# Chunked delta-rule attention and a token-channel mixer: chunks of 64 tokens, 32x32 blocks inverted by substitution on VectorE, head pairs on block-diagonal operands

## The chip, the cores and the metric

The kernel runs on one core of one Trainium2 chip. The metric is device time in microseconds (us), the median of several runs. The engines that appear are PE (TensorE matmul), PEld (its weight loads), DVE (VectorE), ACT (ScalarE), POOL (GpSimd) and SP (SyncE, which here only issues DMAs). All matrix work is fp32, and an fp32 matmul shows in the trace as two instructions, each with its weight load.

## The reference

```python
def _attn_ref(q, k, v, beta):                  # B, H, S, D = 4, 8, 768, 48
    k_n = k / (np.linalg.norm(k, axis=-1, keepdims=True) + 1e-06)
    state = np.zeros((B, H, D, D))
    for t in range(S):
        y[:, :, t] = einsum('bhd,bhde->bhe', q[:, :, t], state)
        v_old = einsum('bhde,bhd->bhe', state, k_n[:, :, t])
        state = state + beta_t * einsum('bhd,bhe->bhde', k_n[:, :, t], v[:, :, t] - v_old)
def _moe_ref(x, w_tok1, w_tok2, w_ch1, w_ch2): # x = y as (4, 768, 384)
    h = np.maximum(x.transpose(0, 2, 1) @ w_tok1, 0.0) @ w_tok2      # 768 -> 256 -> 768
    u = x + h.transpose(0, 2, 1)
    return u + np.maximum(u @ w_ch1, 0.0) @ w_ch2                    # 384 -> 1536 -> 384
```

The weights come as float64 and are rounded to fp32 by the kernel itself, bit by bit.

## The kernel before

The time loop is done in chunks of 128 tokens: 4 batches of 6 chunks, 24 in all, each with its 8 heads. Within a chunk the recurrence becomes a triangular system; its matrix (identity plus a strictly triangular, beta-weighted product of keys) is inverted for each head, and what is left is a chain of small products with the 48x48 states.

Four kinds of work are written as generators and woven into one program.

- `prep` (L262) does what needs no state: it normalises the keys (`ksq`, `ksum`, `knrm`, `kden`, `krec`, `kpad`), transposes keys and queries (`p_t`, L301), forms the triangular products (`p_g`, L313, masked into `gm`, L317) and then inverts. The inversion starts from 2x2 blocks on POOL (`off`, `w_r`, L333 to L338) and doubles the block size five times: per size one 32x32 block transpose on DVE (`t_r`, L345), 16 matmuls of 64x64 by 32 columns (`p_l`, L359), a masked eviction (`lt`, L360), 16 more matmuls (`p_wu`, L372) and a subtraction (`w_r`, L373). A last step (L399 to L416) joins the two 64x64 halves of a chunk.
- `recur` (L420) is the chain through the state: `p_b` (L432), `rhs` (L434), `p_u` (L439), `u` (L441), `p_s` (L447), the new state `st` (L454), and the output `p_y` (L464, L469) into `xb`.
- `mixer` (L476) is the second half of the reference for one batch: `p_1` (L483), `p_h` (L495), then for 256 tokens at a time 12 groups of three matmuls of 128x128 by 256 columns (`p_c`, L517) and 24 of 128x128 by 384 (`p_o`, L529).
- `load_weights` reads 34 pieces of the weights and rounds each with six DVE operations and a POOL addition.

A table of due times (`at(...)`, L562 to L573) orders the program, and the instruction scheduler may move an instruction ahead of others that are not ready. The result is one fixed order for each engine. Attention of batch 0 has nothing beside it but the weights; attention of batches 1 to 3 runs beside the mixer of the batch ahead; the last mixer runs alone.

Of the kernel before, what the change touches and what calls it, by code (L numbers as in the profile page):

```python
# [9 lines left out]
FP32 = mybir.dt.float32  # L10
# [4 lines left out]
C = 128  # L15
DP = 64
R = 64
# [4 lines left out]
def kernel(  # L22
# [26 lines left out]

    nc = tc.nc  # L50
# [11 lines left out]
    GT = 256  # L62
    NG = S // GT
    GC = GT // C
    assert S % GT == 0 and DM % 128 == 0 and DTOK % 128 == 0 and DCH % 128 == 0
    assert D <= DP and H == 8 and BH <= 128

    const = ctx.enter_context(tc.tile_pool(name="const", bufs=1))
    loads = ctx.enter_context(tc.tile_pool(name="loads", bufs=3))
# [6 lines left out]
    def ps_att(shape, name):  # L76
        return psum.tile(shape, FP32, name=name, tag="att", bufs=3)

    def ps_seq(shape, name):
        return psum.tile(shape, FP32, name=name, tag="seq", bufs=2)  # L80
# [7 lines left out]
    mask_u = const.tile([128, 128], FP32, name="mask_u")  # L88
    make_upper_triangular(nc, mask_u, val=1.0, diag=False)

    def pairs(t, s):

        return t.rearrange("p h (n two s) -> p h n two s", two=2, s=s)

    def halves(t, s):

        return t.rearrange("p h (n s) -> p h n s", s=s)

    def folded(name, full, width):

        t = const.tile([128, width], FP32, name=name)
        nc.gpsimd.tensor_copy(out=t, in_=full[:, 0:width])
        for lo in range(width, full.shape[-1], width):
            nc.gpsimd.tensor_tensor(
                out=t, in0=t, in1=full[:, lo : lo + width], op=ALU.add
            )
        return t

    ident_r = folded("ident_r", ident, R)


    mask_f = const.tile([128, 64], FP32, name="mask_f")
    nc.gpsimd.memset(mask_f, 1.0)
    for sign in (1, -1):
        nc.gpsimd.affine_select(
            out=mask_f, in_=mask_f, pattern=[[-2 * sign, 64]], base=0,
            channel_multiplier=sign, compare_op=ALU.is_ge, fill=0.0,
        )
    mask_1 = folded("mask_1", mask_f, R // 2)
# [18 lines left out]
    for i in range(2):  # L138
# [466 lines left out]
```

## Time and profile before

| | |
|---|---|
| median of 3 runs | 1270.54 us (1268.54 to 1272.89) |
| the profiled execution | 1278.59 us, of which the span of the trace is 1276.8 us |
| PE busy | 1169.6 us, 92% of the span |
| DVE, POOL, ACT busy | 431.3, 197.0, 180.7 us |
| packets moved by DMA | 83395, mean 26 GB/s |

A busy time is the union of an engine's instructions. PE's matmuls are pipelined, so a busy PE is not PE at its peak. The granted clock of TensorE has two levels, 1.2 and 2.4 GHz, and a mean of 0.74 in a stretch is a mixture of the two. Until the first record of the clock (at about 80 us here) the column shows 1.00, whatever the level.

### The profile page before, as it was taken

The numbers are of one execution on the slowest core, as the hardware profiler recorded it, in microseconds if no ns is written. First come the engines' busy times: TensorE is split into PE (matmuls) and PEld (weight loads), VectorE is DVE, ScalarE is ACT, GpSimd is POOL, SyncE is SP. The second block draws the span as 40 slices with busy tenths as digits, with TensorE's granted clock in tenths as the row PEclk, the third lists the DMA queues.
The fourth block names the chain that finished last, engine by engine and source line by source line (L and its number), as shares of the span: only waits on it lengthen the run. The fifth ranks groups of instructions, "written<-read, shape, count | busy, mean of one in ns | idle before, by whom it ended". The sixth has DMA issues, their size and how long they took to land.

```text
span 1276.8 us, 27386 instructions
## 1 busy us (share of the span) xinstructions
PE 1169.6 (92%) x12462; PEld 920.6 (72%) x12462; DVE 431.3 (34%) x898; ACT 180.7 (14%) x407; POOL 197.0 (15%) x295
## 2 busy tenths in 40 slices
PE   4788787788999999999999999999999999999998
PEld 3767676677787777777677777777677777786776
DVE  6766674332334323322322313322323322211000
ACT  2001011011111120120121120220121120111111
POOL 6233141111111110110110110110111110000000
PEclk9986575776999999899897998999799999799999
DMA  6232230010001000100000100100000000000000
GB/s 123 79 85 77 70 89 25 14 26 8 15 14 26 21 13 15 32 13 14 20 14 8 32 14 14 32 14 14 20 14 8 14 1 8 7 1 13 13 13 13
DMA packets 83395, 33.31 MB, mean 26 GB/s; under 512 B 75824, under 2 KB 78896, under 8 KB 83280
## 3 DMA queue, kind: packets, MB, share of 16 engines
q1 hardware_dynamic: 83280, 31.56, 10.2%
q8 instruction: 98, 1.61, 0.5%
q14 instruction: 17, 0.14, 0.0%
HBM read 26.84 MB, written 4.72 MB: 25 GB/s over the span
## 4 chain that ended last, share of the span: by engine, by line
PE 86%; DVE 8%; POOL 4%; issue 2%; ACT 0%; POOLq 0%; ACTq 0%
PE p_c L517 15%; PE p_o L529 15%; PE p_l L359 12%; PE p_wu L372 12%; PE p_g L313 4%; PE p_u L439 4%; PE p_y L469 4%; PE p_h L495 3%; PE p_t L301 3%; PE p_l L410 2%; PE p_wu L415 2%; PE p L483 2%; DVE t_r L345 2%; PE p_x L399 2%; POOL off L333 2%
## 5 line engine op out<-in xcount | busy, mean ns | idle before, releaser
L517 PE MATMUL p_c<-u_t,wc 128*128 128x256 f32 x864 | 227.8, 405 | 0.1
L359 PEld LDWEIGHTS p_l<-t_r,gm 64*64 64x64 f32 x3840 | 144.3, 155 | 111.4 <-issue 89.4
L359 PE MATMUL p_l<-t_r,gm 64*64 64x32 f32 x3840 | 157.3, 238 | 65.0 <-DVE t_r L345 60.0
L529 PE MATMUL p_o<-wc,r 128*128 128x384 f32 x576 | 216.8, 507 | 0.0
L372 PEld LDWEIGHTS p_wu<-w_r,lt 64*64 64x64 f32 x3840 | 146.5, 158 | 56.7 <-DVE lt L360 33.0
L517 PEld LDWEIGHTS p_c<-u_t,wc 128*128 128x128 f32 x864 | 159.7, 197 | 25.5 <-issue 2.6
L372 PE MATMUL p_wu<-w_r,lt 64*64 64x32 f32 x3840 | 160.6, 240 | 14.0 <-DVE lt L360 14.0
L529 PEld LDWEIGHTS p_o<-wc,r 128*128 128x128 f32 x576 | 101.2, 191 | 50.9 <-issue 2.9
L360 DVE TENSOR_TENSOR lt<-p_l,mask 128x256 f32<-128x256 f32 x120 | 50.9, 424 | 175.2 <-PE p_l L359 175.0
L317 DVE TENSOR_TENSOR gm<-p_g,mask_u 128x512 f32<-128x512 f32 x96 | 62.0, 685 | 129.3 <-PE p_g L313 129.2
L373 DVE TENSOR_TENSOR w_r<-w_r,p_wu 128x256 f32<-128x256 f32 x120 | 50.6, 421 | 158.8 <-PE p_wu L372 158.6
L345 DVE STREAM_TRANSPOSE t_r<-w_r 128x512 f32<-128x512 f32 x120 | 85.2, 710 | 45.6 <-POOL w_r L338 43.2
L522 ACT ACTIVATE r<-p_c 128x256 f32<-128x256 f32 x144 | 55.2, 383 | 249.6 <-PE p_c L517 249.6
L405 POOL COPY w_t<-w_r 64x512 f32<-64x512 f32 x24 | 15.0, 625 | 455.0 <-DVE w_r L373 455.0
L313 PE MATMUL p_g<-kbq_t,k_t 64*128 64x256 f32 x384 | 64.3, 423 | 3.8 <-DVE gm L317 3.2
L536 DVE TENSOR_TENSOR o_sb<-p_o,xb 128x384 f32<-128x384 f32 x24 | 13.4, 557 | 135.4 <-PE p_o L529 135.4
L313 PEld LDWEIGHTS p_g<-kbq_t,k_t 64*128 64x128 f32 x384 | 41.1, 198 | 20.3 <-DVE gm L317 6.5
L411 ACT COPY lt<-p_l 64x512 f32<-64x512 f32 x24 | 13.9, 580 | 279.6 <-PE p_l L410 279.6
L469 PE MATMUL p_y<-u,gm 128*128 128x48 f32 x384 | 52.1, 289 | 0.0
L469 PEld LDWEIGHTS p_y<-u,gm 128*128 128x128 f32 x384 | 50.0, 207 | 1.9 <-issue 1.0
L333 POOL TENSOR_TENSOR off<-gm,mask 64x256 f32<-64x256 f32 x48 | 36.0, 750 | 78.0 <-DVE gm L317 76.5
L215 POOL TENSOR_TENSOR w_f<-w_f,w_r 128x384 uint32<-128x384 uint32 (+1 forms) x34 | 33.5, 986 | 91.5 <-DVE w_f L207 77.8
(89 smaller groups left out, 1076.5 us busy)
## 6 DMA issues: line engine op xcount, KB each, us to landing
d<-in_moe_w_ch_dram SPq DMA_DIRECT2D x24, 384.0 KB, 3.2
k_raw<-in_k_dram SPq DMA_DIRECT2D x24, 192.0 KB, 2.7
qpad<-in_q_dram SPq DMA_DIRECT2D x24, 192.0 KB, 2.9
v_raw<-in_v_dram SPq DMA_DIRECT2D x24, 192.0 KB, 2.6
out_dram<-o_sb SPq DMA_DIRECT2D x24, 192.0 KB, 1.9
d<-in_moe_w_tok_dram SPq DMA_DIRECT2D x6, 256.0 KB, 3.0
d<-in_moe_w_tok_dram SPq DMA_DIRECT2D x4, 384.0 KB, 3.1
beta_sb<-in_beta_dram SPq DMA_DIRECT2D x1, 96.0 KB, 2.2
```

What stands on the lines that cost most here:

```text
L313: nc.tensor.matmul(p_g[par][:, jj], k_t[lo : lo + DP, j], kbq_t[lo : lo + DP, j])
L317: nc.vector.tensor_tensor(out=gm[:, 4 * g + par : 4 * g + 4 : 2], in0=p_g[par], in1=mask_u[:, None, None, :].to_broadcast([128, 2, 2, 128] ...
L333: nc.gpsimd.tensor_tensor(out=off[lo : lo + R], in0=gm[lo : lo + R, :, 0, lo + 1 : lo + R : 2], in1=mask_1[lo : lo + R, None, :].to_broadc ...
L345: nc.vector.transpose(dst.rearrange("p h n -> p (h n)"), src.rearrange("p h n -> p (h n)"))
L359: nc.tensor.matmul(p_l[r, h], gm[r, h, 0, r], t_e[r, h])
L360: nc.vector.tensor_tensor(out=lt_e, in0=halves(p_l, s), in1=halves(masks[s][:, None, :], s).to_broadcast([128, H, half // s, s]), op=ALU.mult,
L372: nc.tensor.matmul(p_w[r, h], lt[r, h], w_o[r, h])
L439: nc.tensor.matmul(p_u[:, h], w_t[:, h], rhs[:, h])
L469: nc.tensor.matmul(p_y[:, h], gm[:, h, 1], u[:, h], start=(c == 0 and h == 0), stop=(h == H - 1), skip_group_check=True,)
L517: nc.tensor.matmul(p_c, wc1[:, cb, f * 128 : (f + 1) * 128], u_t[:, cb], start=(cb == 0), stop=(cb == NCB - 1),)
L522: nc.scalar.activation(r, p_c, ACTF.Relu)
L529: nc.tensor.matmul(p_o, r2[f][:, i * C : (i + 1) * C], wc2[:, f], start=(f == 0), stop=(f == NHT - 1),)
```

## The change

- **Chunk and unit.** Tokens still come in units of 128 (24 of them, `u`), but the recurrence goes in chunks of 64: two per unit, 48 in all.
- **Head pairs.** The two heads of a pair sit on the two halves of the partitions. One operand of each product is block-diagonal (`kbd`, `r_bd`, `w_bd`, `s_bd`, with zeros off the blocks), so that one 128-row matmul serves both heads. `recur` is three products now: `p_q` (keys and queries with the state), `p_w` (inverse with the right-hand side) and `p_s` (new state and output together), four matmuls each.
- **Inversion.** Units go in rounds of two, 12 rounds. `prep` writes the four diagonal 32x32 blocks of each matrix to DRAM (`n_dram`), `invert` reads them back with one block on each of 64 partitions (`x`), and runs 30 steps of back substitution on DVE, a product and a sum each: 60 operations, each dependent on the one before, on 30 to 240 elements per partition, 9920 elements in all. The inverse and its transpose (`xt`, by POOL) go to DRAM again, and 16 small DMAs bring them to the places where the matmuls read them (`wt`, `t11`, `w22`). `join` then makes the off-diagonal 32x32 block of each 64x64 inverse with 16 matmuls (`p_z`, `p_x`) and four ACT copies.
- **Mixer.** `p_c` takes 128 tokens at a time, four groups of 128 columns to a PSUM tile; the transposition of the next 128 tokens (`turn`) stands ahead of `p_o`.
- **Weights.** Three DVE operations per piece instead of six; two ACT operations take over the rest.
- **DMAs.** All on SP's queue, in order. There are 638 of them now; before there were 131.

```diff
-C = 128
+C = 64
+U = 128
+HB = 32
+RU = 2
...
+        nc.scalar.activation(r, lo, ACTF.Copy, scale=2.0**-29)
+        nc.scalar.square(a, hi.bitcast(FP32))
...
+        kst = work.tile([128, NP, 2, D], FP32, name="kst", bufs=1)
+        for par in range(2):
+            for cc in range(2):
+                nc.sync.dma_start(
+                    out=kst[C * par : C * par + C, :, cc],
+                    in_=kp[C * cc : C * cc + C, par::2, 0:D],
+                )
...
+        for g in range(2):
+            p_g = ps_prep([128, NB // 2, 2, C], "p_g")
+            for i in range(NB // 2):
+                nb = g * (NB // 2) + i
+                nc.tensor.matmul(p_g[:, i], kbd[0][:, nb], kqt[:, nb])
...
+        for par in range(2):
+            for i in range(2):
+                lo = (4 * j + 2 * par + i) * NB
+                row = C * par + HB * i
+                nc.sync.dma_start(
+                    out=xins[rnd][lo : lo + NB].rearrange("b s t -> s b t"),
+                    in_=gm[row : row + HB, :, 2, HB * i : HB * i + HB],
+                )
...
+    def invert(rnd):
...
+        x = work.tile([n, HB, HB], FP32, name="x")
+        nc.sync.dma_start(out=x, in_=n_dram)
+        yield
+        for s in range(1, HB - 1):
+            w = HB - 1 - s
+            tmp = work.tile([n, s, w], FP32, name="sub")
             nc.vector.tensor_tensor(
+                out=tmp, in0=x[:, 0:s, s : s + 1].to_broadcast([n, s, w]),
+                in1=x[:, s : s + 1, s + 1 : HB].to_broadcast([n, s, w]), op=ALU.mult,
+            )
+            nc.vector.tensor_tensor(
+                out=x[:, 0:s, s + 1 : HB], in0=x[:, 0:s, s + 1 : HB], in1=tmp,
+                op=ALU.add,
             )
             yield
...
+        nc.sync.dma_start(out=w_dram, in_=x)
+        nc.sync.dma_start(out=t_dram, in_=xt)
...
+    def join(u):
...
+            nc.tensor.matmul(p_z[0:65, nb], gm[:, lo : lo + 65], t11[:, nb])
...
+            nc.tensor.matmul(p_x[0:65, nb], zst[:, lo : lo + 65], w22[:, nb])
...
     def recur(t):
...
+                nc.tensor.matmul(p_q[:, p], kqt[:, 2 * p + cc], s0[:, p])
+            for r, e in heads:
+                nc.vector.tensor_tensor(
+                    out=r_bd[r, :, e], in0=v_st[r, :, cc], in1=p_q[hi, :, e],
+                    op=ALU.subtract,
+                )
...
+                p_w[0 : C + 1, p], wts[u % NV][:, w_lo : w_lo + C + 1], r_bd[:, p]
+            )
+        for r, e in heads:
+            nc.scalar.copy(w_bd[r, :, e], p_w[lo, :, e])
...
+            nc.tensor.matmul(p_s[:, p], gm[:, 2 * p + cc, 0:2], w_bd[:, p])
...
+        at(t0 - 2.9 + j, 0.08, prep, u)
+        if j == 0:
+            at(t0 - 1.4, 0.9 / (HB + 2), invert, rnd)
+        at(u - 0.9, 0, load_v, u)
+        at(t0 - 0.4 + 0.2 * j, 0.1, join, u)
+        for cc in range(2):
+            at(u + 0.5 * cc, 0.15, recur, 2 * u + cc)
```

What moves in the fixed orders is shown at three places.

PE before, beside the mixer of batch 0: the small matmuls of one inversion (`p_l`, `p_wu`) alternate with two or three matmuls of the mixer.

```order
L359 MATMUL p_l<-t_r,gm 64x32 x16
L517 MATMUL p_c<-u_t,wc_159 128x256 x2
L372 MATMUL p_wu<-w_r,lt_128 64x32 x16
L517 MATMUL p_c<-u_t,wc_159 128x256 x3
L359 MATMUL p_l<-t_r,gm 64x32 x16
L517 MATMUL p_c<-u_t,wc_159 128x256 x2
L372 MATMUL p_wu<-w_r,lt_130 64x32 x16
```

PE after, the end of the mixer's stretch between two rounds and the start of the next round's join and recurrence, beside the mixer of batch 0:

```order
L497 MATMUL p_ut<-ident,xb 128x128 x3
L528 MATMUL p_o<-wc_137,r_2845 128x384 x3
L392 MATMUL p_z<-t_0_115,gm_95 65x64 x8
L528 MATMUL p_o<-wc_137,r_2845 128x384
L528 MATMUL p_o<-wc_137,r_2892 128x384
L403 MATMUL p_x<-w_0_119,zst_123 65x64 x8
L528 MATMUL p_o<-wc_137,r_2892 128x384 x2
L442 MATMUL p_w<-r_bd_125,wt_107 65x96 x4
L528 MATMUL p_o<-wc_137,r_2892 128x384
L451 MATMUL p_s<-w_bd_127,gm_95 128x96
L392 MATMUL p_z<-t_1_116,gm_96 65x64 x8
```

The alternation is gone: a long stretch of mixer work comes first, and then the join and the four chunks of a round stand close together, with single matmuls of the mixer between them.

DVE after, in the same kind of round: the last two chunks of a round, and then the substitution of the next round.

```order
L455 TENSOR_TENSOR s_bd_130<-s_bd_129,p_s 64x4x48 x2
L461 TENSOR_TENSOR xb<-xb,p_s 64x384
L312 TENSOR_TENSOR gm_95<-p_g,mb 128x4x2x64
L429 TENSOR_TENSOR r_bd_125<-v_st,p_q 64x4x48 x2
L344 TENSOR_TENSOR sub<-x 64x30
L348 TENSOR_TENSOR x<-x,sub 64x30
L344 TENSOR_TENSOR sub<-x 64x58
L348 TENSOR_TENSOR x<-x,sub 64x2x29
```

The substitution begins behind the right-hand side (`r_bd`) of the round's last chunk, whenever its input `x` has come.

SP after, from the stores of one round's blocks to the loads that the next join waits for:

```order
L327 DMA n_dram<-gm_98 32x8x32 x4
L278 DMA kst<-kpad_86 64x4x48 x3
L339 DMA x<-n_dram 64x1024
L278 DMA kst<-kpad_86 64x4x48
L216 DMA kpad_85<-in_k_dram 128x8x48
L327 DMA n_dram<-gm_95 32x8x32 x4
L227 DMA v_st<-in_v_dram 64x4x48 x4
L216 DMA qpad_89<-in_q_dram 128x8x48
L278 DMA kst<-kpad_85 64x4x48 x4
L358 DMA w_dram<-x 64x1024
L359 DMA t_dram<-xt 64x1024
L369 DMA wt_109<-w_dram 32x8x32 x2
```

Before, the queue held nothing here but the loads of `k_raw`, `qpad` and `v_raw`, one at a time, and the stores of `o_sb`.

## Rows read from the trace of the kernel before

**Rows 1.** The page: busy time, share of the span, instructions; all DMA packets.

```profile
PE 1169.6 (92%) x12462; PEld 920.6 (72%) x12462; DVE 431.3 (34%) x898; ACT 180.7 (14%) x407; POOL 197.0 (15%) x295
DMA packets 83395, 33.31 MB, mean 26 GB/s; under 512 B 75824, under 2 KB 78896, under 8 KB 83280
```

**Rows 2.** Three stages: length, busy time and instructions per engine, granted clock, DMA.

```profile
0.00:320.00 320.00, 241.81 (x2806) 215.34 (x2806) 177.15 (x393) 35.49 (x70) 92.38 (x143) 0.74 0.24 59
320.00:1161.00 841.00, 816.22 (x9238) 626.08 (x9235) 246.88 (x492) 127.36 (x290) 104.64 (x152) 0.96 0.07 15
1161.00:1276.80 115.80, 111.58 (x427) 79.22 (x425) 7.23 (x13) 17.83 (x47) 0.00 (x0) 1.00 0.03 12
```

**Rows 3.** Groups by line: busy us, mean ns | idle before, releaser.

```profile
L517 PE MATMUL p_c<-u_t,wc 128*128 128x256 f32 x864 | 227.8, 405 | 0.1
L359 PE MATMUL p_l<-t_r,gm 64*64 64x32 f32 x3840 | 157.3, 238 | 65.0 <-DVE t_r L345 60.0
L372 PE MATMUL p_wu<-w_r,lt 64*64 64x32 f32 x3840 | 160.6, 240 | 14.0 <-DVE lt L360 14.0
```

**Rows 4.** Timeline of PE (start, length): one inversion step, early and beside a mixer.

```profile
26.04 1.92 PE L372 MATMUL p_wu<-w_r,lt 64*64 64x32 f32 x32 [0.61 <-DVE lt L360]
397.50 1.12 PE L372 MATMUL p_wu<-w_r,lt 64*64 64x32 f32 x32
```

**Rows 5.** Last mixer: timeline (first row), chain that ended last (other rows).

```profile
1168.77 8.11 PE L495 MATMUL p_h<-r,w 128*128 128x384 f32 x24
...
1210.14 15.54 PE p_c L517 x72
1225.68 15.48 PE p_o L529 x48
```

**Rows 6.** Timeline of PE: full-width weights with few columns.

```profile
1042.83 1.89 PE L439 MATMUL p_u<-rhs,w_t 128*128 128x48 f32 x16
1044.65 1.14 PE L313 MATMUL p_g<-kbq_t,k_t 64*128 64x256 f32 x8
...
431.72 1.03 PE L447 MATMUL p_s<-u,kpad 128*128 128x96 f32 x8
...
65.10 1.86 PE L447 MATMUL p_s<-u,kpad 128*128 128x96 f32 x8
```

**Rows 7.** DVE operations by tile (ns min/median/max), and a dependent pair in the timeline.

```profile
L281 DVE TENSOR_TENSOR kpad<-k_raw,krec x24: 557/559/1089, 7.3 to 1055.9; 128x384 f32<-128x384 f32 x24
L278 DVE TENSOR_SCALAR kden<-knrm x24: 126/164/784, 6.3 to 970.1; 128x8 f32<-128x8 f32 x24
L280 DVE RECIPROCAL krec<-kden x24: 159/202/203, 7.1 to 970.2; 128x8 f32<-128x8 f32 x24
L454 DVE TENSOR_TENSOR st<-st,p_s x32: 307/352/358, 124.0 to 1103.7; 64x192 f32<-64x192 f32 x32
...
1105.24 0.42 DVE L373 TENSOR_TENSOR w_r<-w_r,p_wu 128x256 f32<-128x256 f32 x1 [1.14 <-PE p_wu L372]
1105.69 0.71 DVE L345 STREAM_TRANSPOSE t_r<-w_r 128x512 f32<-128x512 f32 x1
```

**Rows 8.** Groups by line: an eviction on ACT, a copy on POOL.

```profile
L441 ACT COPY u<-p_u 128x384 f32<-128x384 f32 x24 | 11.5, 479 | 51.0 <-PE p_u L439 51.0
L405 POOL COPY w_t<-w_r 64x512 f32<-64x512 f32 x24 | 15.0, 625 | 455.0 <-DVE w_r L373 455.0
```

**Rows 9.** DMAs: SP's issue (ns, then timeline), us to landing on the page.

```profile
L251 SPq DMA_DIRECT2D k_raw<-in_k_dram x24: 367/368/1080, 1.3 to 963.9; - x24
...
4.21 0.86 SPq L251 DMA_DIRECT2D qpad<-in_q_dram  x1
79.09 34.05 SPq L193 DMA_DIRECT2D d<-in_moe_w_ch_dram  x8
...
k_raw<-in_k_dram SPq DMA_DIRECT2D x24, 192.0 KB, 2.7
out_dram<-o_sb SPq DMA_DIRECT2D x24, 192.0 KB, 1.9
```

More of the change, by code (lines that the diff above doesn't have):

```diff
@@ L87 @@
     make_identity(nc, ident)
[L88 to L107, printed above, removed]
@@ L293, in prep @@
+        bd = blocks(kbd[0])
+        nc.scalar.copy(kqt_k, p_t)
+        nc.scalar.copy(bd[0:DP, :, :, 0:C], p_t[0:DP])
+        nc.gpsimd.tensor_copy(
+            out=bd[DP : 2 * DP, :, :, C : 2 * C], in_=kqt_k[DP : 2 * DP]
         )
         yield
[L296 to L303 removed]
@@ L367, in step @@
             yield
-            p_w = ps_att([128, H, half], "p_wu")
-            for h in range(H):
-                for lo in range(0, 128, size):
-                    r = slice(lo, lo + size)
-                    nc.tensor.matmul(p_w[r, h], lt[r, h], w_o[r, h])
-            nc.vector.tensor_tensor(
-                out=w_o, in0=w_o, in1=halves(p_w, s), op=ALU.subtract
+        rnd, j = divmod(u, RU)
+        if j == 0:
+            xins[rnd] = dram.tile([RU * 4 * NB, HB, HB], FP32, name="n_dram")
@@ L393, in prep @@
-        yield from step(32, 64, w_6, t_6)
-        lo_r, hi_r = slice(0, 64), slice(64, 128)
-        p_x = ps_att([64, H, 32], "p_x")
-        for h in range(H):
-            nc.tensor.matmul(p_x[:, h], w_6[lo_r, h], lt_buf[32][lo_r, h, 0:32])
-        nc.vector.tensor_tensor(
-            out=t_6[lo_r, :, 0:32], in0=t_6[lo_r, :, 0:32], in1=p_x, op=ALU.subtract
-        )
-        w_t = work.tile([128, H, 128], FP32, name="w_t")
-        nc.gpsimd.memset(w_t[hi_r, :, 0:64], 0.0)
-        nc.gpsimd.tensor_copy(out=w_t[lo_r, :, 0:64], in_=w_6[lo_r])
@@ L406, in prep @@
-        nc.gpsimd.tensor_copy(out=w_t[hi_r, :, 64:128], in_=w_6[hi_r])
-        yield
-        p_l = ps_att([128, H, 64], "p_l")
-        for h in range(H):
-            nc.tensor.matmul(p_l[hi_r, h], gm[lo_r, h, 0, hi_r], t_6[lo_r, h])
-        nc.scalar.copy(lt_buf[64][hi_r], p_l[hi_r])
-        yield
-        p_w = ps_att([64, H, 64], "p_wu")
-        for h in range(H):
-            nc.tensor.matmul(p_w[:, h], lt_buf[64][hi_r, h], w_6[hi_r, h])
-        nc.scalar.mul(w_t[lo_r, :, 64:128], p_w, -1.0)
+        nc.vector.memset(x.rearrange("b s t -> b (s t)")[:, 0 :: HB + 1], 1.0)
@@ L437, in recur @@
[L437 to L452 removed]
+            p_q = ps_seq([128, NP, 2 * D], "p_q")
@@ new lines, in recur @@
+            for p in range(NP):
+                nc.tensor.matmul(p_q[:, p], kqt[:, 2 * p + cc], s0[:, p])
[3 more added lines that the diff above has]
+                    op=ALU.subtract,
+                )
+            nc.scalar.mul(y, p_q[lo], -1.0)
+        else:
+            for r, e in heads:
+                nc.gpsimd.tensor_copy(out=r_bd[r, :, e], in_=v_st[r, :, cc])
+        yield
@@ L462, in recur @@
         if c > 0:
[L463 to L473 removed]
+            nc.vector.tensor_tensor(out=y, in0=y, in1=p_s[lo], op=ALU.add)
+        else:
+            nc.scalar.copy(y, p_s[lo])
```

495 lines of the change are left out of this document (235 added, 260 removed).

## The prediction

> **What bounds the kernel now.** I read the page first: PE is busy for 92% of the span [rows 1], so the question is what PE does and at which clock. The stages answer it [rows 2]. In the first 320 us (attention of batch 0 and the weights) PE is busy for 242 us, at a mean granted clock of 0.74; in the next 841 us (attention of batches 1 to 3 beside mixers 0 to 2) it is busy for 816 us at 0.96; in the last 116 us (mixer 3) for 112 us at 1.00. The groups by line show what fills this [rows 3]: 7680 of PE's 12462 instructions are the 64x64 products `p_l` and `p_wu` of the inversion, 318 us of busy time, and `p_l` waits 65 us more for the transposes. One step of 32 takes 1.92 us early in the run and 1.12 us beside a mixer [rows 4]: the two levels of the clock, 1.2 and 2.4 GHz. So the middle is bound by PE's own work, the head by the chain of one inversion after another, and the tail by one mixer.
>
> **PE's work after the change, at full clock.** An instruction with a full-width weight load costs about 114 ns however few columns it has: 16 of `p_u` fill the 1.82 us between their start and the next row's, and 8 of `p_s` take about 1.0 us (1.86 us early in the run) [rows 6]. Per unit: 8 transposes and 16 instructions of `p_g`, 24 x 0.114 = 2.7 us; 32 of `p_z` and `p_x`, with 65 columns of weights, which the trace lacks: between 0.033 us (a step of 32 in about 1.05 us [rows 4]) and 0.114 us each, taken as 0.08, 2.6 us; two chunks with 16 of `p_q` and `p_s` at 0.125 and 8 of `p_w` at 0.08, 5.3 us. That is 10.6 us, 21 us per round of two units. A mixer: 48 instructions of `p_1` and `p_h`, 15.8 us (24 took 8.11 [rows 5]); per unit 24 of `p_o`, 7.7 us (48 in 15.48), and 72 of `p_c`. These have half the columns of before, so the floor is half of 215.8 ns (72 in 15.54), 108 ns, and the weight load sets 114: 8.2 us against 7.8. With 0.3 us of transposes a unit's share is 18.9 us, a round's 38. PE's floor is therefore 59 us per round; 841 us for 18 units was 93 us per two units.
>
> **The loop that replaces it.** A round cannot start before its inverse is there, and its blocks come out of the round ahead. By the orders the loop runs: join, chunks 0 to 3 up to the last right-hand side, substitution on DVE, two trips through DRAM, next join.
>
> (a) Join to the last `r_bd`. A hop between engines is 0.03 to 0.15 us in the rows [rows 7]. The join has two groups of 16 matmul instructions (1.3 us each) and two pairs of ACT copies of 256 elements; 384 take 479 ns [rows 8], so I take 0.4 each: 4.2 us. A chunk is `p_q` 1.0, two DVE operations of 0.35 (192 elements [rows 7]), `p_w` 0.65, two ACT copies of 0.32, `p_s` 1.0, two DVE operations of 0.35, and six hops: 5.3 us. Three chunks, and `p_q` and `r_bd` of the fourth: 21.8 us in all. The second join, two units' `prep` (4.6 us of PE for transposes and `p_g`) and single mixer matmuls stand between these in PE's queue; I charge 6 us of them as not hidden. 28 us.
>
> (b) Substitution. 384 elements took 559 ns, 8 elements 164 to 202 [rows 7]: 155 ns and 1.04 ns per element. A dependent operation starts 0.03 us after the end of the one ahead [rows 7]. 60 x 0.185 + 9920 x 0.00104 = 11.1 + 10.3 = 21.4 us. The low end is 10 us (the fixed part wholly hidden, which no row shows for dependent operations), the high end 27 (if short broadcast rows cost half as much again per element); I take 21.4, because the dependent pair is this very case. Between these operations DVE's order has a chunk's state and output, a key normalisation and two to six additions for the mixer, some 5 us. 26.5 us. The Trainium skill, page "VectorE: DVE Perf Modes", section "The TRN2 errata — SBUF-src ops pay a fixed extra latency per instruction", speaks against this step: many small operations pay the fixed cost each time, and tiles should have 512 elements or more. Its cycle table would give 58 cycles fixed at 0.96 GHz, an estimate of 14 us for the 60; the same section corrects this to about 150 cycles, which agrees with the 559 ns.
>
> (c) The way back. POOL's transposed copy of 1024 elements, 1.2 us (512 took 625 ns [rows 8]), the store of it (issue 0.37, landing 1.9), eight loads issued at 0.37 each, 3.0 us, and the landing of the last, 2.3, between 1.9 and 2.7 [rows 9]: 8.8 us.
>
> The way out (`gm`, four stores, a load of `x`: about 9 us) starts at `p_g`, about 14 us after the join, and is over at about 23 us, before `r_bd` of the last chunk: it costs nothing as long as (a) is longer. Where it is late, DVE's order makes the substitution later by as much. The loop is 28 + 26.5 + 8.8 = 63 us, above PE's floor of 59; with some of it at the low clock I take **64 us**. The mixer's stretch of about 28 us in PE's queue covers (b) and (c) but for a few us, so this stretch is nearly free.
>
> **The sum**, against the profiled execution. *Until the first join, 84 us.* SP issues 16 loads of beta (16 x 0.37) and four of keys and queries at about 0.9 us each, where SP is backed up [rows 9]; the first keys are there at about 10 us. Normalisation 3, two units through one `kbd` 14: 27 us. Way out 6.5, and then the substitution with ten weight pieces in between in DVE's order. Eight pieces took 34 us before [rows 9], with six DVE operations each; now there are three, so ten take between 30 and 43; I take 42 us for both together, since a piece that comes late holds the substitution behind it. Way back 8.8. *Two loops in the head* at the low clock, where (a) is 32 us: 32 + 42 + 9 = 83 with weights, and 32 + 28 + 9 = 69 without. *Nine loops* at 64: 576. *The last round's chunks* 32. *The last mixer* 109: from `p_h` to the end took 108 [rows 5], six groups of `p_c` cost 0.4 more each, and `turn` ahead of `p_o` takes away a wait or two. 84 + 83 + 69 + 576 + 32 + 109 = 953 us of span. The profiled execution was 1.8 us longer than its span and 0.6% above the median: 955 x 1270.54 / 1278.59 = 949, which I give as **950 us**.
>
> **Rivals.** (1) *PE is the bound.* If the operations of the substitution overlap, or the trips are shorter, nine loops cost 59 each and the head loses some 20 us: 953 - 45 - 20 = 888, or 884 us; 904 where the head stays. For it: floor and loop are 4 us apart. Against it: the dependent pair [rows 7].
> (2) *The low clock in the chunks.* PE waits a few us ahead of each join, and then works with gaps of 0.7 us in every chunk. The head shows what such gaps go with: steps at 1.92 us and a clock of 0.74 [rows 2, 4]; the middle, nearly without gaps, had 0.96. At 1.2 GHz the products in (a) take some 10 us longer: loops of 74, 90 us more, 1038 us. The Trainium skill ("TensorE: Matmul & The Clock Gate", part 1) says the same as a rule: the throttled clock is the default, and only sustained activity lifts it. Against it: the long stretch of mixer matmuls in each round.
> (3) *Slower than before: the small DMAs.* 18 to 22 issues of 128 to 192 byte pieces lie on each loop. The time is as before when a loop takes 100 us ((1276.8 - 84 - 83 - 69 - 141) / 9), 36 us more, nearly 2 us for each of these DMAs. This would happen if they ran one behind the other up to their landing. Against it: a load of 1024 pieces of 192 bytes is issued in 0.86 to 1.08 us where they queue up [rows 9], so 256 pieces should not need more than the 0.37 us of the issue; and 75824 of 83395 packets were under 512 bytes before [rows 1]. From 1275 us.
> (4) *The change does not do what it says.* The wide matmuls bring nothing where the weight load is the cost: this is in the sum already, at 114 ns for 48 to 128 columns.
>
> **How the numbers follow.** The forecast (loops of 61 to 69 us, 925 to 995 us) 0.50; rival 1 (865 to 925) 0.25; rival 2 (995 to 1085) 0.18; rival 3 0.03; faster than 865 by a shorter head as well, 0.04. The low end takes PE's floor and a head 35 us shorter (30 in place of 42 us in the two substitutions with weights, 11 us less in the third): 953 - 45 - 35 = 873, 867 us. The high end takes loops of 74 and a head 20 us longer (all of it at the low clock): 1065, 1058 us. Range 865 to 1060; what is left out is below 865, rival 3 and the upper part of rival 2, about 1 in 10. A measurement of this kernel tells 0.3% from no change; only rival 3 reaches that: faster 0.96, same 0.01, slower 0.03.
>
> **What would show it.** Right: PE busy near 600 to 700 us and not over 80% of the span; 720 substitution operations of 190 to 440 ns on DVE, about 250 us; joins 60 to 68 us apart once a mixer runs, with `p_z` waiting for the DMA of `t11` or `wt`; `p_c` at about 114 ns; mixer 3 about 109 us from `p_h` on. Wrong: joins 59 us apart with no wait on PE (rival 1); `p_s` at 1.8 us for 8 beside a mixer (rival 2); DMAs on SP's queue with landings well above 3 us, or the substitution waiting for `x` and not for `r_bd`; a first join far from 84 us.

## The result, and the profile after

The changed kernel takes **918.75 us** (median of 4 runs, 912.34 to 923.02); beside it the kernel before took 1271.72 us. The ratio is 0.7215, with a 95% interval of 0.7162 to 0.7268. The prediction was 950 us, range 865 to 1060. The profiled execution took 917.84 us, its span is 916.1 us. Of all executions told of below one, the longest of `warm2`, fell into a slower state at a lower granted clock, and its time is left out.

The page of the changed kernel, to be read against [rows 1]:

```profile
PE 735.6 (80%) x5034; PEld 594.5 (65%) x5034; DVE 473.3 (52%) x1254; ACT 232.5 (25%) x535; POOL 138.3 (15%) x150
...
PEclk9555875695699999999999999999999999989999
DMA packets 192354, 56.06 MB, mean 61 GB/s; under 512 B 182560, under 2 KB 185632, under 8 KB 192288
...
L348 DVE TENSOR_TENSOR x<-x,sub 64x30 f32<-64x30 f32 (+4 forms) x360 | 124.1, 345 | 9.9
L344 DVE TENSOR_TENSOR sub<-x 64x30 f32<-64x30 f32 (+4 forms) x360 | 120.3, 334 | 16.8 <-DMA x<-n_dram 7.6
```

PE has 434 us less work. The 7680 small products of the inversion are gone [rows 3], and 720 operations of the substitution on DVE (244 us) stand in their place. There are 2.3 times as many packets. The stages (length, busy time and instructions of PE, PEld, DVE, ACT, POOL, then the granted clock, DMA share and GB/s), against [rows 2]:

```profile
0.00:87.00 87.00, 16.13 (x74) 13.80 (x75) 65.31 (x149) 26.66 (x58) 43.17 (x56) 0.66 0.59 128
87.00:165.40 78.40, 29.02 (x217) 24.62 (x217) 56.06 (x135) 26.31 (x59) 24.61 (x21) 0.67 0.45 111
165.40:227.70 62.30, 29.00 (x216) 24.56 (x216) 36.11 (x100) 13.66 (x34) 9.09 (x9) 0.72 0.31 64
...
355.28:415.18 59.90, 59.16 (x421) 47.79 (x422) 34.01 (x95) 15.94 (x37) 7.16 (x7) 1.00 0.31 61
...
774.80:916.10 141.30, 131.02 (x792) 101.45 (x792) 13.14 (x28) 20.88 (x45) 0.00 (x0) 0.96 0.04 13
```

The windows are cut at the joins (the first `p_z` of a round). In the head PE is busy for a fifth to a half of the time, and DVE for three quarters while there are weights. In the middle a round of 59.90 us holds 59.16 us of busy PE at the full clock. The joins of the changed kernel and of the variants below, in us from the start of the span (each has twelve):

| kernel | joins 1, 2, 3 | mean of the nine rounds from join 3 to join 12 | last join to the end |
|---|---|---|---|
| changed kernel | 87.0, 165.4, 227.7 | 60.8 | 141.3 |
| `sub20` (ten steps less) | 69.2, 137.6, 202.2 | 54.0 | 167.5 |
| `sub40` (ten steps twice) | 87.6, 168.1, 243.8 | 64.9 | 141.0 |
| `back` (shorter way back) | 85.2, 162.1, 225.3 | 60.0 | 142.3 |
| `mix256` (256 tokens to a `p_c`) | 87.1, 165.6, 227.8 | 60.6 | 144.6 |
| `early` (inversion a unit earlier) | 85.9, 159.1, 232.5 | 54.0 | 175.6 |
| `after_w6` (six-op rounding) | 89.3, 173.7, 253.7 | 60.3 | 139.0 |
| `warm` / `warm2` (unread matmuls) | 99.4, 196.4, 282.5 / 92.9, 181.1, 252.7 | 60.1 / 60.0 | 141.3 / 141.2 |
| `best1` (inversion ahead, tuned head) | 87.8, 122.9, 196.7 | 54.5 | 175.6 |

One round on four engines (start, length). PE: the join that begins it, which waits, the mixer's last stretch, and the next join.

```profile
355.28 1.13 PE L392 MATMUL p_z<-t,gm 128*65 128x64 f32 x16 [0.72 <-DMA t<-t_dram]
...
399.40 8.20 PE L513 MATMUL p_c<-u_t,wc 128*128 128x128 f32 x72
407.44 7.91 PE L528 MATMUL p_o<-wc,r 128*128 128x384 f32 x24
415.18 1.11 PE L392 MATMUL p_z<-t,gm 128*65 128x64 f32 x16
```

DVE: the last right-hand side of the round that began at 355.28, the first operation of the substitution, a dependent pair, and the last operation.

```profile
379.94 0.74 DVE L429 TENSOR_TENSOR r_bd<-v_st,p_q 64x192 f32<-64x192 f32 x2
...
381.19 0.17 DVE L344 TENSOR_TENSOR sub<-x 64x30 f32<-64x30 f32 x1
...
394.61 0.40 DVE L344 TENSOR_TENSOR sub<-x 64x240 f32<-64x240 f32 x1
395.04 0.40 DVE L348 TENSOR_TENSOR x<-x,sub 64x240 f32<-64x240 f32 x1
...
406.46 0.20 DVE L348 TENSOR_TENSOR x<-x,sub 64x30 f32<-64x30 f32 x1
```

The way back: POOL's transposed copy, and SP's issues, of which the second load of `t11` (413.02) is the last that the first `p_z` needs.

```profile
406.73 1.96 POOL L355 COPY xt<-x 64x1024 f32<-64x1024 f32 x1 [22.18 <-DVE x L348]
```

```profile
406.69 0.48 SPq L358 DMA_DIRECT2D w_dram<-x  x1
408.71 0.48 SPq L359 DMA_DIRECT2D t_dram<-xt  x1
...
413.02 0.45 SPq L378 DMA_DIRECT2D t<-t_dram  x1
```

So this round is 25.9 us from the join to the substitution, 25.5 us of substitution, 8.5 us of way back. That is the prediction's loop. But `p_z` shows no wait at its end: PE comes out of `p_o` 2.2 us behind the issue of that load. In four of the nine rounds `p_z` waits for it, for 0.3 to 0.7 us, and starts 1.9 to 2.1 us behind the issue; so here, too, the data lands as PE becomes free. Loop and PE end together, and the trace alone does not tell which of them sets the round. The experiments were made for that, and for the head.

### The profile page after: what moved, and what is told of

Its sections match the earlier page's. It is cut to its first block, busy times and chain, and to the rows that moved or that the text cites. A ratio compares the mean times of both kernels' runs of the same rounds, so it can differ in the third digit from the quotient of the medians.

```text
span 916.1 us, 13640 instructions
## 1 busy us (share of the span) xinstructions
PE 735.6 (80%) x5034; PEld 594.5 (65%) x5034; DVE 473.3 (52%) x1254; ACT 232.5 (25%) x535; POOL 138.3 (15%) x150
## 4 chain that ended last, share of the span: by engine, by line
PE 58%; DVE 19%; DMA 7%; ACT 5%; issue 4%; POOL 3%; SPq 3%; POOLq 0%; ACTq 0%; DVEq 0%
PE p_c L513 14%; PE p_o L528 13%; DVE x L348 6%; DVE sub L344 6%; PE p_s L451 6%; PE p_q L427 4%; PE p_w L442 4%; PE p_h L487 4%; PE p_g L310 3%; PE p_z L392 3%; PE p L475 3%; PE p_x L403 3%; ACT w_bd L446 3%; DMA t_dram<-xt 2%; DMA t<-t_dram 1%
## 5 line engine op out<-in xcount | busy, mean ns | idle before, releaser
L513 PE MATMUL p_c<-u_t,wc 128*128 128x128 f32 x1728 | 202.6, 276 | 2.3 <-ACT u_t L501 2.3
L528 PE MATMUL p_o<-wc,r 128*128 128x384 f32 x576 | 196.7, 488 | 0.0
L348 DVE TENSOR_TENSOR x<-x,sub 64x30 f32<-64x30 f32 (+4 forms) x360 | 124.1, 345 | 9.9
L344 DVE TENSOR_TENSOR sub<-x 64x30 f32<-64x30 f32 (+4 forms) x360 | 120.3, 334 | 16.8 <-DMA x<-n_dram 7.6
L451 PE MATMUL p_s<-w_bd,gm 128*128 128x96 f32 x384 | 58.8, 296 | 11.1 <-ACT w_bd L446 8.6
L451 PEld LDWEIGHTS p_s<-w_bd,gm 128*128 128x128 f32 x384 | 50.5, 203 | 22.8 <-ACT w_bd L446 22.8
L310 PE MATMUL p_g<-kqt,kbd 128*128 128x128 f32 x384 | 56.8, 297 | 6.9 <-POOL kbd L292 4.7
L310 PEld LDWEIGHTS p_g<-kqt,kbd 128*128 128x128 f32 x384 | 51.1, 208 | 13.5 <-POOL kbd L292 13.3
L427 PEld LDWEIGHTS p_q<-s_bd,kqt 128*128 128x128 f32 x352 | 44.3, 194 | 17.9 <-DVE s_bd L455 5.7
L427 PE MATMUL p_q<-s_bd,kqt 128*128 128x96 f32 x352 | 49.8, 282 | 7.2 <-DVE s_bd L455 7.0
L442 PE MATMUL p_w<-r_bd,wt 128*65 128x96 f32 x384 | 43.2, 257 | 5.0 <-DVE r_bd L429 2.5
```

Source lines behind the costliest of these rows:

```text
L310: nc.tensor.matmul(p_g[:, i], kbd[0][:, nb], kqt[:, nb])
L344: nc.vector.tensor_tensor(out=tmp, in0=x[:, 0:s, s : s + 1].to_broadcast([n, s, w]), in1=x[:, s : s + 1, s + 1 : HB].to_broadcast([n, s, w ...
L348: nc.vector.tensor_tensor(out=x[:, 0:s, s + 1 : HB], in0=x[:, 0:s, s + 1 : HB], in1=tmp, op=ALU.add,)
L427: nc.tensor.matmul(p_q[:, p], kqt[:, 2 * p + cc], s0[:, p])
L442: nc.tensor.matmul(p_w[0 : C + 1, p], wts[u % NV][:, w_lo : w_lo + C + 1], r_bd[:, p])
L451: nc.tensor.matmul(p_s[:, p], gm[:, 2 * p + cc, 0:2], w_bd[:, p])
```

## The experiments

In all of them the rest of the program is the changed kernel's, except in `before_w3`. The times are medians.

**1. Ten substitution steps less.**

```diff
-        for s in range(1, HB - 1):
+        for s in [*range(1, 11), *range(21, HB - 1)]:
```

> Leaves out 10 of the 30 substitution steps (s = 11 to 20, the longest ones), so the inverse is not the inverse; all else is as in the changed kernel. A step takes 0.85 us there, so each loop has 8.5 us less on DVE. Theory A (the round is the loop: join, chunks, substitution, trip through DRAM): joins in the middle 60.8 - 8.5 = 52 us apart, the head 14 + 17 us shorter: about 811 us. Theory B (PE's own work sets the middle, with a floor of 58 to 59 us): joins 58 to 59.5 us apart, p_z without a wait, only the head falls: 870 to 890 us.

Measured: 857.99 us (857.57 to 858.32), between the two forecasts; each theory is right in one place. The joins 4 to 9 come 50.3 to 52.8 us apart, some 8 us less as the loop says, and well below the 58 us that theory B held for PE's floor. The whole is 61 us faster and not 107: the nine rounds give 6.8 us each and not 8.5, the head 26 us, and the end takes 26 back. What PE does between two joins had changed. In the round shown it ran 144 instructions of `p_c` in both kernels, but fewer of `p_o` (over the nine rounds 1152 of `p_c` for 1296, and 368 of `p_o` for 432). PE's `p_o` alone in that round (length, busy and instructions of PE and PEld), first of the changed kernel, then of this one:

```profile
355.28:415.18 59.90, 22.80 (x66) 11.85 (x66) 1.00 0.31 61
```

```profile
312.18:364.31 52.13, 15.41 (x43) 7.29 (x42) 1.00 0.36 69
```

The mixer's work that had stood between the joins is done behind the last one, 167.5 us there against 141.3. The same view of this kernel's end, with all instructions (PE, PEld, DVE, ACT, POOL):

```profile
688.30:855.80 167.50, 163.46 (x1014) 128.46 (x1012) 15.53 (x33) 25.33 (x53) 0.00 (x0) 1.00 0.05 14
```

So the fixed order lays as much mixer work between two joins as fits into the loop that it was made for, and the backlog is worked off at the end. PE's own floor, spread over the nine rounds, is by this run about (486.2 + 167.5 - 141.3) / 9 = 56.9 us.

**2. Ten steps twice.**

```diff
+            if 11 <= s <= 20:
+                again = work.tile([n, s, w], FP32, name="again", bufs=1)
+                nc.vector.tensor_tensor(out=again, in0=x[:, 0:s, s:s+1]..., in1=tmp, op=ALU.mult)
+                nc.vector.tensor_tensor(out=again, in0=again, in1=tmp, op=ALU.add)
```

> Does 10 of the 30 substitution steps (s = 11 to 20) once more, on a scratch tile, so each loop has about 8.5 us more on DVE and the result is the same. Theory A (the loop is the bound): joins in the middle 69 us apart, the whole 14 + 11 x 8.5 = about 105 us longer, 1020 to 1030 us. Theory B (PE is the bound and the loop has slack): the middle moves by less than the 8.5 us; with all the slack that the five rounds without a wait could hide (several us) joins 62 to 65 us apart, 960 to 1000 us.

Measured: 970.37 us (968.61 to 970.50), rounds of 64.9 us. That is in theory B's interval, for a reason that neither theory had. Twenty more operations of 0.39 us cost 4.1 us per round, not 8.5. DVE of this kernel:

```profile
415.10 0.39 DVE L344 TENSOR_TENSOR sub<-x 64x234 f32<-64x234 f32 x1
415.41 0.38 DVE L358 TENSOR_TENSOR again<-again,sub 64x228 f32<-64x228 f32 x1
415.72 0.39 DVE L348 TENSOR_TENSOR x<-x,sub 64x234 f32<-64x234 f32 x1
416.03 0.39 DVE L354 TENSOR_TENSOR again<-x,sub 64x234 f32<-64x234 f32 x1
416.34 0.39 DVE L344 TENSOR_TENSOR sub<-x 64x238 f32<-64x238 f32 x1
```

The operations now alternate between two chains, and each starts 0.31 us behind the one ahead, before that one has ended. In the changed kernel the same operations depend on each other and start 0.43 us apart. A step of four costs 1.24 us, a step of two 0.87: 10 x 0.37 = 3.7 us, near the 4.1 by which the rounds grew. The rounds followed DVE's chain by its real cost, so theory A's mechanism holds for a longer loop too, and its expectation was mis-sized. PE's order followed as well, though the edit adds nothing but DVE operations: in the same round it holds 164 instructions of `p_c` and these of `p_o`:

```profile
377.45:440.91 63.46, 24.91 (x72) 12.91 (x72) 1.00 0.31 61
```

**3. One part of the change alone, in the kernel before: three operations per weight piece.**

```diff
-        nc.vector.scalar_tensor_tensor(out=f, in0=lo, scalar=29, in1=f, ...)
-        nc.vector.tensor_scalar(out=r, in0=lo, scalar1=28, ...)
-        nc.vector.tensor_scalar(out=e, in0=hi, scalar1=20, ...)
+        nc.scalar.activation(r, lo, ACTF.Copy, scale=2.0**-29)
+        nc.scalar.square(a, hi.bitcast(FP32))
```

> The kernel before with one part of the change alone: three DVE operations and two ACT operations per piece of the weights, in place of six on DVE. Theory A (weights cost the head because their DVE operations stand between those of the inversion): 34 pieces with 3 operations of some 0.4 us less each, 41 us of DVE time, of which a half shows: 1245 to 1260 us. Theory B (the head of before is a chain through PE and its evictions, and the weights lie beside it): within 5 us of 1270.

Measured: 1273.95 us, ratio 0.9993 (0.9968 to 1.0017): nothing, theory B. DVE has 137.3 us of work in the first 320 us there instead of 177.2 [rows 2], and the 40 us less moved nothing, so they were not on the path.

**4. The same part undone in the changed kernel** (the same diff, backwards).

> The changed kernel with the rounding of the weights as before: six DVE operations per piece instead of three, and none on ACT. Theory A (in the head of the changed kernel DVE is the path, so what stood between its operations counts): about 24 of the 34 pieces lie between substitution operations of the first two rounds; 3 operations of 0.4 to 0.5 us more each, 30 to 35 us longer: 945 to 960 us. Theory B (as in the kernel before, where the same edit alone gave nothing: the additions on POOL and the arrival of the pieces set the pace): within 6 us of 919.

Measured: 938.28 us (937.30 to 942.99), 19.5 us slower. The three head joins come 2.3, 8.3 and 26.0 us later; some 6 us are given back behind them. So the part is worth 20 us here and nothing before; the reading is that the substitution, the other part of the change, has put DVE on the path of the head. Theory A was right in kind; it had 30 to 35 us, and the head lost 26. But not where it said: the first two substitutions hardly grew (42.8 and 39.9 us for 41.3 and 39.7). The weights ended later, the last DVE operation on them starting at 243.4 us and not at 184.9, so that they stand between the operations of the third substitution as well: it took 37.7 us, and 24.5 in the changed kernel, which has none of them there.

**5. The mixer of before.**

```diff
-                p_c = ps_mlp([128, FG, 128], "p_c")
+                p_c = ps_mlp([128, GT], "p_c")        # GT = 256
```

> The changed kernel with the mixer of before: 256 tokens to a product p_c, so half as many instructions of 256 columns. Theory A (weight load of 114 ns against 108 ns of columns, PE on the path in the middle): 1728 x 6 ns, about 10 us less PE time, 907 to 912 us. Theory B (PE is not on the path but for the last mixer): 1 to 3 us less at most; the transposition that no longer stands ahead of p_o may give that back: 915 to 922 us.

Measured: 917.95 us (914.81 to 921.57), theory B. The rounds gain 0.1 to 0.2 us, the end loses 3.3.

**6. A shorter way back.**

```diff
-        nc.gpsimd.tensor_copy(out=xt, in_=x.rearrange("b s t -> b t s"))
+        nc.vector.tensor_copy(out=xt, in_=x.rearrange("b s t -> b t s"))
```

and per unit the loads in the order four of `wt`, two of `t11`, two of `w22`.

> The changed kernel with a shorter way back: the transposed copy xt by DVE instead of POOL (1.96 us there; about 1.2 by the rate of the substitution's operations), and the loads of t11 and w22 issued ahead of those of wt (the second t11 is two places earlier, 0.9 us). Theory A (the way back is on the loop): 1.5 to 1.9 us less in each of eleven rounds, 898 to 903 us. Theory B (mixer work in PE's queue fills the round): joins in the middle move by less than 0.5 us, 912 to 917 us.

Measured: 909.12 us (905.27 to 909.94), between the two intervals. The first two joins gain 1.8 and 1.5 us, the third gives 0.8 back; the middle gains 0.8 us per round on average, almost half of it in the first. One round shows why it is not more. The last operation of the substitution ends at 400.0 us. The second `t11` is issued 5.3 us behind that (it was 6.4; it is the sixth load in both kernels, so the reordering gave less than expected). With the 2.2 us from issue to join of the changed kernel (413.02 to 415.18) it has landed by about 407.6. PE comes to `p_z` at 408.57, out of the same 24 `p_o`:

```profile
404.91 0.89 SPq L376 DMA_DIRECT2D t<-t_dram  x2
```

```profile
400.83 7.91 PE L526 MATMUL p_o<-wc,r 128*128 128x384 f32 x24
408.57 1.11 PE L390 MATMUL p_z<-t,gm 128*65 128x64 f32 x16
```

The order on PE is the one made for the longer loop (144 `p_c` and 67 `p_o` between these joins), so PE's queue sets the round now. Theory B for the middle but for its first round, theory A for the first two joins. DVE's copy took 1.06 us where POOL's took 1.96.

**7. The inversion a unit earlier.**

```diff
-        at(t0 - 2.9 + j, 0.08, prep, u)
+        at(t0 - 3.9 + j, 0.08, prep, u)
-            at(t0 - 1.4, 0.9 / (HB + 2), invert, rnd)
+            at(t0 - 2.4, 0.9 / (HB + 2), invert, rnd)
```

(the loads a unit earlier as well; the weights begin a unit earlier and are spread over a unit more; `NV = 5`, one buffer of `x`, for room)

> The changed kernel with one thing moved: loads, prep and invert are planned one unit (128 tokens) earlier, with five buffers of gm, kqt and wt instead of four (x has one buffer instead of two, for room). No operation is added or left out. Theory A (the substitution needs only keys; it is the order of the program that ties it to the chunks and makes a loop of the round, and without that PE's own work is the bound): no wait of p_z in the middle, the second and third joins come 30 to 40 us earlier together, and the whole is set by PE's work, as in the run with ten steps left out: 830 to 860 us. Theory B (the round is a loop whatever the plan, since DVE's queue, DRAM trips and buffers follow the chunks): 905 to 925 us.

Measured: 894.87 us (893.93 to 896.04), faster than theory B had it and 35 us above theory A's interval. In the middle it is theory A: `p_z` waits for 0.45 us at most, rounds are 54.0 us on average, and the mixer's backlog stands behind the last join (the last two stages, from join 4 to join 12 and from there to the end):

```profile
295.50:718.70 423.20, 415.45 (x3112) 347.44 (x3111) 259.89 (x735) 120.97 (x285) 51.71 (x52) 1.00 0.32 62
718.70:894.30 175.60, 171.55 (x1072) 135.52 (x1070) 16.79 (x36) 27.66 (x59) 0.00 (x0) 1.00 0.04 12
```

From the third join to the end it takes 661.8 us, with ten steps less it took 653.7, in the changed kernel 688.4. So the substitution is not tied to the chunks by data; `prep` and `invert` need keys and beta only. The plan had tied it. The head did not gain: the second join is 6 us earlier, but the third 5 us later. Two things in the trace make for that, and no run takes them apart. DVE's order puts the second substitution behind the state of the first chunk, for which it waits (the load of its `x` was issued at 90.37 us):

```profile
97.70 0.73 DVE L459 COPY s_bd<-p_s 64x192 f32<-64x192 f32 x2 [11.58 <-PE p_s L451]
98.47 0.18 DVE L344 TENSOR_TENSOR sub<-x 64x30 f32<-64x30 f32 x1
```

And the weights, spread further by the same edit, lie in the third substitution: their last DVE operation starts at 227.7 us instead of 184.9, and that substitution takes 51.8 us instead of 24.5.

**8 and 9. The head's clock: unread matmuls beside the first three substitutions.** First `warm`, then `warm2`; the way back has twelve more, of 512 columns of `x` and of `ident` by `ident`.

```diff
+                for _ in range(2 if s % 2 else 1):
+                    nc.tensor.matmul(p_k, ident[0:n], tmp.rearrange("b s w -> b (s w)"))
```

```diff
+                nc.tensor.matmul(p_k[:, 0:w], ident[0:n], tmp[:, 0])
+                for _ in range(2):
+                    nc.tensor.matmul(p_k, ident, ident)
```

> The changed kernel with matmuls that nobody reads, beside the substitutions and the way back of the first three rounds (46 and 12 to each), so that PE is busy there. Theory A (the low clock in the head costs: PE's 74 us of work in the first 228 us would take two thirds of that, and the chunks between joins 26 us instead of 30): granted clock in the head above 0.9, 10 to 20 us less, 900 to 909 us. Theory B (hops, DVE and DMA set the head): within 4 us of 919. Theory C (the extra matmuls hold up the work behind them in PE's queue): 922 us and more.

> As the run with unread matmuls beside the first three substitutions, but fewer and shorter ones: two of 128x128 by 128 columns (identity by identity, all 128 rows) and one short one on 64 rows per step, twelve of them on the way back (at most 6 us at the low clock), so that none stands in front of a join. In the changed kernel the granted clock is 0.50 until some 10 us behind each join of the head and 0.9 to 1.0 after that. Theory A (the clock in these 10 us is what it costs): granted clock 1.00 at the joins, 4 to 5 us less in each of three rounds, 904 to 909 us. Theory B (the clock stays at 0.50 as beside the 64-row matmuls, or the first products after a join are set by their hops): 916 to 924 us.

Measured: 966.67 us (962.54 to 967.01) and 930.71 us (922.27 to 935.49, three executions). `warm` is theory C: its last matmuls hold PE until 99.4 us, and the join stands behind them.

```profile
78.60 20.82 PE L368 MATMUL p_k<-x,ident 64*128 64x512 f32 x24
99.36 2.02 PE L404 MATMUL p_z<-t,gm 128*65 128x64 f32 x16
```

`warm2` is theory B on the clock, and slower than B had it: PE was busy throughout and the clock stayed low all the same until 92.2 us, so that these matmuls, too, ran late into the join (92.9 against 87.0). They also held the substitutions: DVE waited 8.0 us for those that read `tmp` before it could write it anew, and the first two substitutions took 45.3 and 49.1 us instead of 41.3 and 39.7.

```profile
36.00:60.00 24.00, 23.60 (x84) 19.69 (x84) 19.29 (x51) 5.77 (x13) 7.77 (x7) 0.50 0.68 149
60.00:87.00 27.00, 27.00 (x98) 23.00 (x98) 23.57 (x56) 6.96 (x15) 10.60 (x9) 0.50 0.47 118
...
92.20:99.00 6.80, 4.36 (x52) 3.92 (x52) 0.00 (x0) 2.07 (x6) 0.00 (x0) 1.00 0.60 148
```

What the low clock costs in the head stays open. In the changed kernel it is low for 12 us behind each of the first two joins and 18 us behind the third, and high after that; behind the first:

```profile
87.00:97.00 10.00, 7.54 (x52) 6.92 (x53) 0.36 (x1) 2.06 (x6) 0.00 (x0) 0.50 0.46 110
97.00:107.00 10.00, 8.90 (x82) 8.03 (x81) 5.82 (x13) 7.52 (x18) 3.32 (x4) 0.91 0.30 59
```

Some of it can be read from the time between a join and the next substitution. Behind the first join of the changed kernel it is 29.6 us with 12 us of low clock, behind the first two of `warm2` 28.0 us with 7 and 31.3 us with 17; behind the first of `warm`, 32.4 us with 14. So the low clock goes with a few us in a round, and other things go into these times too.

**10. A faster version.** `early` with the way back of experiment 6, two buffers of `x` (room from `wt`, `tmp`, `o_sb` and masks), the first keys among beta's loads, and

```diff
-        at(t0 - 3.9 + j, 0.08, prep, u)
+        at(t0 - 4.15 + j, 0.08, prep, u)
-            at(t0 - 2.4, 0.9 / (HB + 2), invert, rnd)
+            at(t0 - 2.7, 0.9 / (HB + 2), invert, rnd)
```

> As the run that plans prep and invert a unit earlier, but the inversion 0.3 units earlier still, with two buffers of x, so that the second substitution follows the first on DVE at once instead of behind the first chunk's state; the way back by DVE and with t11 ahead of wt; the first keys loaded among beta's loads instead of behind them. Theory A (the head is then DVE's work, and after the third join PE's work alone, 654 to 662 us as in the runs with ten steps left out and with everything earlier): joins at about 80, 118 and 160 us, 815 to 830 us. Theory B (the weights, rounded until about 225 us as before, hold the first mixer, or DVE holds the chunks behind the substitution): third join at 200 us or later, 855 to 885 us.

Measured: **864.09 us** (862.18 to 866.42), ratio to the kernel before 0.6788 (0.6739 to 0.6836), 6% faster than the changed kernel. That is theory B's interval, with the third join 3 us ahead of where B had it. The second substitution now follows the first at once:

```profile
80.24 0.20 DVE L348 TENSOR_TENSOR x<-x,sub 64x30 f32<-64x30 f32 x1
80.47 1.03 DVE L355 COPY xt<-x 64x1024 f32<-64x1024 f32 x1
81.42 0.17 DVE L344 TENSOR_TENSOR sub<-x 64x30 f32<-64x30 f32 x1
```

and the second join comes at 122.9 instead of 165.4. But the third comes only at 196.7, since the third substitution starts at 144. Two reasons offer themselves in the program and the trace, and neither was shown: it needs a fifth and sixth unit prepared, and there are five buffers; and its load of `x` stood on SP's queue behind two weight pieces that waited for theirs:

```profile
127.40 9.61 SPq L168 DMA_DIRECT2D d<-in_moe_w_ch_dram  x2
137.19 0.47 SPq L339 DMA_DIRECT2D x<-n_dram  x1
```

**11. That version without ten steps** (the diff of experiment 1).

> The version with the inversion planned ahead (864 us) without 10 of its 30 substitution steps (s = 11 to 20), so the inverse is not the inverse; in the changed kernel itself the same edit took 61 us off. Theory A (with the inversion ahead, PE's own work is the bound behind the head, and DVE's in the head): from the fourth join to the end 620 to 630 us as with all steps (626), and only the head shorter, by up to three times 8.5 us: 838 to 852 us. Theory B (the substitution still sets the pace of the rounds): 8.5 us less in each of eight rounds more, 800 us or less.

Measured: 844.82 us (844.78 to 848.70), in theory A's interval, though not where it put the gain. The fourth join is the same (236.3 against 237.0 us), the fifth is 24 us earlier, and from there on nothing is gained. The stage from the fifth join to the end, without the steps and with them:

```profile
286.25:843.00 556.75, 552.50 (x3912) 456.58 (x3910) 201.00 (x551) 136.12 (x313) 31.27 (x39) 1.00 0.23 46
```

```profile
310.10:863.00 552.90, 542.14 (x3841) 447.43 (x3839) 246.71 (x662) 133.45 (x308) 30.08 (x38) 1.00 0.22 44
```

PE is busy for 98 to 99% of it in both, and 46 us of DVE's work less (201 against 247) makes nothing shorter. It is this second observation that makes PE the bound there.

**12. That version with the load of `x` on ACT's queue.**

```diff
-        nc.sync.dma_start(out=x, in_=n_dram)
+        nc.scalar.dma_start(out=x, in_=n_dram)
```

> The version with the inversion planned ahead (864 us), with one edit: the load of x is issued on ACT's queue instead of SP's. There two weight pieces stood on SP's queue from 127.4 to 137.0 us, waiting for their buffers, and the load of x for the third substitution behind them, though n_dram was stored by 127.3. Theory A (SP's order in the head is on the path): the third substitution starts 6 to 9 us earlier and the end comes as much earlier, 853 to 858 us. Theory B (DVE is full in the head, so a substitution that starts earlier only pushes the weights back; or ACT now waits for n_dram with copies behind it): within 4 us of 864, or slower.

Measured: 879.70 us (878.33 to 880.41), 15.6 us slower, which theory B allowed for, and no answer: the edit changed the order on all engines. One more weight piece stood between the operations of the first substitution, the load of `x` for the third was issued at 148.5 us instead of 137.2, and that substitution began at 153 us. The question of SP's order in the head stays open.

## Why the prediction was right where it was, and where it was not

The sum, part by part:

| part | predicted, us | measured, us |
|---|---|---|
| until the first join | 84 | 87.0 |
| head loop with weights | 83 | 78.3 |
| head loop without | 69 | 62.4 |
| nine loops | 576 | 547.1 |
| last round's chunks and last mixer | 141 | 141.3 |
| span | 953 | 916.1 |

**Direction and size.** The time lies inside the range, 3% under the forecast, and 29 of the 37 us of span are the nine loops. It lies below the forecast's own interval of 925 to 995 us and in that of rival 1 (865 to 925), to which the prediction gave 0.25.

**PE's work** was priced well. 72 `p_c` take 8.04 us from start to start of what follows (407.44 - 399.40): 112 ns each, taken as 114. 16 `p_z` took about 0.95 us where they run beside the mixer, 0.06 each and not 0.08. The floor of 59 us per round is 57 by experiment 1. Rival 4 was right to be in the sum: with 256 columns nothing is gained (experiment 5).

**The loop.** (a) 25.9 instead of 28 us, (b) 25.5 instead of 26.5, (c) 8.5 instead of 8.8. (The hops in (a) are put down to [rows 7], which has them on one engine only.) In (b) the 60 operations are 244 / 12 = 20.4 us, predicted 21.4; the pair of 240 elements is 0.40 us, 0.43 from start to start, as the dependent pair of [rows 7] had it. The Trainium skill, page "VectorE: DVE Perf Modes", section "The TRN2 errata — SBUF-src ops pay a fixed extra latency per instruction", puts the fixed part at about 150 cycles at 0.96 GHz, and the trace agrees: 0.40 us for 240 elements less 240 cycles of 1.04 ns leave 0.15 us. In (c) errors of both signs cancel: POOL's copy is 1.96 us and not 1.2 (it was priced by a copy of rows of [rows 8], and this one turns each block), and an issue on SP is 0.45 us and not 0.37; but the load that is waited for is the sixth of the eight. The mean round is 60.8 us; the 64 us also held a share for the low clock, and the granted clock was 1.00 in every round of the middle but two (0.84 in the first, 0.97). Rival 2 did not happen.

**The step that failed** is the sentence that a round cannot start before its inverse, whose "blocks come out of the round ahead", and with it the choice between forecast and rival 1. The prediction took loop and PE's floor for two bounds of which one wins, and had them 4 us apart. They are coupled: the order on PE changes with the length of DVE's chain and fills the round with mixer work up to it (in one and the same round 43 instructions of `p_o` with ten steps less, 66 in the changed kernel, 72 with ten steps twice), so PE shows as busy and `p_z` as nearly free of waits at any length of the loop. Of what a shorter loop gives at the joins, a part is paid back at the end, and behind the head PE's work is what remains (experiments 1, 7, 11). And the loop is not one of data: nothing but the plan puts the substitution behind the chunks (experiment 7).

**The head.** 42 us for the first substitution with its weights were 41.3 (36.7 to 78.0 us), and 39.7 in the second round. The head loops' other parts were 29.6 us to the substitution, not 32, and the substitution without weights was 24.5 us, not 28. The first join is 3 us late because the substitution starts at 36.7 us, where the sum had 27 + 6.5 = 33.5.

**What would show it.** PE's busy time is 735.6 us, not 600 to 700, with the 80% at the line. The sign did not fit the prediction's own sum: nine rounds at 59 us, three in the head at 21, the last round's chunks at 16 and a mixer of 109 make 719. 720 operations, 244 us, in the middle 0.17 to 0.40 us each but for a few that POOL held: as said. Joins 58 to 67 us apart, but with waits of `p_z` in four rounds only, and short ones: half as said, and this was the sign of the coupling. Mixer 3 from `p_h` (805.8 us) to the end: 110 us, predicted 109. Rival 3 did not come: the load of `t11` is there about 2 us behind its issue, and a round of 60 us with 2.3 times the packets is far from the 100 us that it wanted. In the low end of the range the step from span to time was left out: 873 us gives 869, not 867.

## What to carry to other kernels

Where an order is fixed ahead of the run, an engine that is busy all round long is no proof that its work is the bound: shorten the other chain, and see whether the joins move and where the work turns up again. Ask of every loop whether data or only the plan closes it; here moving the inversion ahead took 24 us off, and with the way back and the head's order changed as well 55, without any operation less. And an edit that brings nothing in one kernel (the three-operation rounding) can be worth 20 us in the next, once another part has put its engine on the path.

## What the runs showed of the hardware

- **DVE operations overlap when they are independent.** Dependent ones of 0.40 us start 0.43 us apart, alternating ones of 0.39 us 0.31 apart (experiment 2): 0.12 us less for each.
- **An operation of the substitution is held while POOL works.** In the head of the changed kernel an addition that takes 0.39 us elsewhere took 1.07, and ended just behind a POOL addition. Eight such are in the first substitution, of 0.73 to 1.15 us, and each ended 0.1 to 0.3 us behind POOL's operation:

```profile
52.01 1.07 DVE L348 TENSOR_TENSOR x<-x,sub 64x228 f32<-64x228 f32 x1
```

```profile
51.82 1.01 POOL L184 TENSOR_TENSOR w_f<-w_f,w_r 128x384 uint32<-128x384 uint32 x1 [4.19 <-DVE w_f L180]
```

  The Trainium skill, page "SBUF — State Buffer", section "🔬 SBUF: two separate sides", says that DVE operations with two SBUF inputs and POOL share a pair of ports under a lock for a whole instruction; the 1.07 us agree with that.
- **The granted clock stayed at 0.50 (1.2 GHz) for 51 us of a busy PE** (experiment 9, 36 to 87 us), in which PE ran products of the identity by itself and a short one for each step. It rose at 92.2 us there, while the last of the identity's products ran (24 instructions in 4.83 us from 88.19 on), and at 98.8 us in the changed kernel, with the join and the first chunk's products ahead of it. The Trainium skill ("TensorE: Matmul & The Clock Gate", part 1) has activity release the throttle; here 50.6 us of busy time in 51 did not, and the measurement decides. What did is not settled by these runs.
